# Logits of tiles 12 and 13 by matmuls, a denser order of the early routing's steps, two buffers for the copies of transposed tiles

## The chip, the core and the metric

One NeuronCore of a Trainium2 chip runs the whole program. The metric is the device time of one execution in microseconds; of a kernel the median of its runs is taken. TensorE does matmuls and transposes, VectorE and ScalarE the elementwise work, GpSimd elementwise work and the issue of some DMAs, SyncE the issue of the other DMAs. Each engine takes its instructions in the order in which the program gives them; where one needs another's result it waits on a semaphore, and everything behind it on that engine waits too.

## The reference

Three layers follow each other on 2304 tokens of width 512: a linear attention with a norm for each head, a dense mixture of 4 experts, and a mixture of 8 experts in which each token goes to one.

```python
kv  = einsum('bhsd,bhse->bhde', k, v)
out = einsum('bhsd,bhde->bhse', q, kv)
x   = out / sqrt(mean(out*out, -1) + 1e-6) * g_norm          # -> (2304, 512)
p   = domain_probs / (domain_probs.sum(-1) + 1e-9)
x   = sum_e p[:, e] * (relu(x @ w1[e]) @ w2[e])              # 4 experts, all tokens
xn, en = x / (|x| + 1e-6), emb / (|emb| + 1e-6)
logits = xn @ en.T / tau                                     # 2304 x 8
idx    = argmax(logits, 1);  gate = softmax(logits)[idx]
out[idx == e] = gate * (relu(x[idx == e] @ w1b[e]) @ w2b[e]) # 8 experts
```

## The kernel before

**Tiles.** A tile is 128 tokens, 18 in all (0 to 17); a unit is three tiles, u0 to u5. Tiles 12 to 14 are the fifth unit, u4, tiles 15 to 17 the last, u5. Fp32 operands are split into a high and a low part (`split`: ScalarE casts the high part, as `w1h`, `w2h`, `xth`; VectorE subtracts, as `w1l`, `w2l`, `xtl`, L62), and each product is three matmuls.

**The dense layer** goes expert by expert. A *phase* takes one unit (or a pair, by a Strassen scheme) through one half `fh` of the hidden width. The last four phases belong to the last expert and go (u4, fh0), (u4, fh1), (u5, fh1), (u5, fh0). Each has four *plain steps* (`plain_unit`, L802: 12 matmuls of 128x384; then ScalarE writes `hh`, VectorE `hl`) and six *L2 steps* (`l2_unit`, L909: 6 matmuls of 128x512), two for each tile, part 0 and part 1. Behind part 1 VectorE adds the product to the tile's sum `acc` (L918). When a tile has its last expert's last half (u4 in its fh1, u5 in its fh0) this is final: GpSimd's queue writes the row to `x1d` in DRAM, and a generator for the tile's logits is put into the list `bg`. For tiles 15 to 17 the sum goes to a buffer of its own, `fin`.

**Logits** come in two ways. `logits_v` reads the row back by a DMA from `x1d` and makes eight multiply-reduce operations on VectorE (L314). `logits_t` squares the row on ScalarE, transposes it with four TensorE transposes into `pslt` (L324), copies it to `xx` on ScalarE (L325), and after a `yield` makes the logits by matmuls with 8 columns into `psl` (L329).

**Early routing.** `route_a` stands in `bg` behind the logits of tile 14 and routes the first 15 tiles (TA = 15) while u5 is still in the dense layer: `pick` (largest logit, one-hot `oh`), `ranks` (prefix counts by matmuls, `psr`, L393), `experts` (`e_int`, the expert of each slot, for which SyncE's weight loads of the slots wait), `places`, the gates, then `invert`. `invert` makes the table of which token is in which slot: VectorE writes five one-hot tiles `po` at a time, TensorE multiplies them in `psi` (L454), and VectorE copies the result to `gs` and `ix`. `psl`, `psr` and `psi` share one PSUM buffer (tag `kv`). `route_b` does the like for the last three tiles, later.

**What sets the order.** After each step of a phase `background(pace)` runs so many pieces of the generators in `bg`, up to their next `yield`. A `yield` of a positive number w ends the call and lets the next w calls pass; a `yield -1` only ends the call. The pace is a list, one number a step; after the last phase the rest runs until four slots' stakes are set. The attention of later tiles lies in the phases of the dense layer too: `att` lists units for a tile (`qt_unit` with `psq`, `xt_unit` with `psxt` of the tile before, `x_unit` with `psx`, `x_norm` with VectorE's `xs`), and `spread` puts them at equal distances over a phase.

**The routed layer** takes slots of 128 gathered tokens: GpSimd gathers rows `xg` (L711, by `ix`), TensorE transposes them (`pstx`, L1170), multiplies (`psm`, L1180), transposes the hidden part (`psth`, L1191) and multiplies again (`psy`, L1202). Its weights go through the same split; VectorE's and ScalarE's splits of the first slots are emitted where the program comes to them, between the generators' pieces.

Of the kernel before, what the change touches and what calls it, by code (L numbers as in the profile page):

```python
# [8 lines left out]
F32 = mybir.dt.float32  # L9
# [11 lines left out]
def attn_moe_moe_kernel(ctx: ExitStack, tc: tile.TileContext, q, k, v, g_norm, dprobs, w1, w2, emb, tau, w1b, w2b, out):  # L21
# [4 lines left out]
    D = H * DH  # L26
# [4 lines left out]
    NC = D // 128  # L31
# [3 lines left out]
    TS = SUB // 128  # L35
# [40 lines left out]
    late = {}  # L76
# [101 lines left out]
    def x_norm(t):  # L178
        ps, xs, st = x_rt.pop(t)
        ri = rms_end(*st)  # L180
        nc.vector.tensor_tensor(out=xs, in0=ps, in1=ri.unsqueeze(2).to_broadcast([128, H, DH]), op=ALU.mult)
        x_s[t] = xs
# [33 lines left out]
    TA = 5 * TS  # L216
# [100 lines left out]
            yield 0  # L317

    def logits_t(t, x):
        xx = late["tmp"].tile([128, NC, 128], F32, name="xx", tag="xx")  # L320
        nc.scalar.activation(out=xx.rearrange("p c n -> p (c n)"), in_=x, func=ACTF.Square, accum_out=ssq[:, t:t + 1])
        ps = psp.tile([128, NC, 128], F32, name="pslt", tag=f"x{t % 2}" if t < NT - 1 else nxt("l2"))
        for c in range(NC):
            nc.tensor.transpose(ps[:, c], x[:, 128 * c:128 * c + 128], ident)  # L324
        nc.scalar.copy(xx, ps)  # L325
        yield -1
        pl = psp.tile([128, E2], F32, name="psl", tag="kv")
        for c in range(NC):
            nc.tensor.matmul(out=pl, lhsT=xx[:, c], rhs=en_t[:, c], start=(c == 0), stop=(c == NC - 1))  # L329
        nc.vector.tensor_copy(lg[:, t], pl)  # L330
        yield 0
# [96 lines left out]
    def invert(t1, k0, n, slot):  # L428
        sh = [128, t1, n]
        g = slice(0, t1)  # L430
        so, rhs = tmp(sh, "so", BF16), tmp([128, t1, 5, n], "rhs", BF16)
        gp, ga, gb = tmp([128, 3, t1], "gp", BF16), tmp([128, t1], "ga"), tmp([128, t1], "gb")
        nc.vector.tensor_copy(gp[:, 0], gate[:, g])
        tt(ga, gate[:, g], gp[:, 0], ALU.subtract)
        nc.vector.tensor_copy(gp[:, 1], ga)
        tt(gp[:, 2], ga, gp[:, 1], ALU.subtract)
        tt(so, bc(slot, sh, 2), bc(lane[:, 0:n], sh, 1), ALU.is_equal)
        yield 0
        for i, a in enumerate((ids[:, 0, g], ids[:, 1, g], gp[:, 0], gp[:, 1], gp[:, 2])):
            tt(rhs[:, :, i], so, bc(a, sh, 2), ALU.mult)  # L440
            yield 0
        yield 3
        ps = psp.tile([128, 5, n], F32, name="psi", tag="kv")
        pend = []
        t0 = 0
        while t0 < t1 or pend:
            m = min(R, t1 - t0)
            po = None
            if m:
                po = late["tmp"].tile([128, R, 128], BF16, name="po", tag="po", bufs=2)  # L450
                for i in range(m):
                    ts(po[:, i], lane_b, pos[:, t0 + i:t0 + i + 1], ALU.is_equal)
            for t, w in pend:
                nc.tensor.matmul(  # L454
                    out=ps.rearrange("p a k -> p (a k)"), lhsT=w, rhs=rhs[:, t].rearrange("p a k -> p (a k)"), start=(t == 0), stop=(t == t1 - 1)
                )
            pend = [(t0 + i, po[:, i]) for i in range(m)]
            t0 += m
            yield -1
        sl = slice(k0, k0 + n)  # L460
        nc.vector.tensor_copy(gs[:, sl], ps[:, 0])
        nc.vector.scalar_tensor_tensor(out=ix[:, sl], in0=gs[:, sl], scalar=PAD, in1=ps[:, 1], op0=ALU.add, op1=ALU.add)
        nc.vector.tensor_copy(gs[:, sl], ps[:, 2])
        for i in (3, 4):
            tt(gs[:, sl], gs[:, sl], ps[:, i], ALU.add)
        yield 0
# [431 lines left out]
    def l2_unit(t, e, fh, part, i, first):  # L898
        if part == 0:
            ps2[0] = bank(i)  # L900
        ps = ps2[0]
        u, n = divmod(t % (2 * TS), TS)
        ns = slice(128 * n, 128 * n + 128)
        fs = (0, 1, 3, 2)
        for k in (2 * part, 2 * part + 1):
            f = fs[k]
            j, a = divmod(f, 2)
            for m, (o, w) in enumerate(((0, w2h), (0, w2l), (1, w2h))):
                nc.tensor.matmul(out=ps, lhsT=h_t[o][f][u][:, ns], rhs=w[j][:, a], start=(k == 0 and m == 0), stop=(k == 3 and m == 2))  # L909
        if part == 0:  # L910
            return
        ac = acc[t % len(acc)]
        last = e == E1 - 1 and fh == ((t // TS) % 2 == 0 or t < N // 128 - 2 * TS)
        if first:
            nc.scalar.activation(out=ac, in_=ps, func=ACTF.Copy, scale=dp[:, t, 0:1])
        else:
            fin = late["tmp"].tile([128, D], F32, name="fin", tag="fin", bufs=3) if last and t >= TA else ac
            nc.vector.scalar_tensor_tensor(out=fin, in0=ps, scalar=dp[:, t, e:e + 1], in1=ac, op0=ALU.mult, op1=ALU.add)  # L918
            ac = fin
        if last:  # L920
            nc.gpsimd.dma_start(out=x1d[128 * t:128 * t + 128, :], in_=ac)
            bg.append((logits_v if t < TA - 1 else logits_t)(t, ac))
            if t == TA - 1:
                bg.append(route_a())
            if t == NT - 1:
                bg.append(route_b())

    bg, rest = [], [0]
# [32 lines left out]
    def att(tiles):  # L961
        u, prev = [], None
        for t in tiles:
            u.append(lambda t=t: qt_unit(t))
            if prev is not None:
                u.append(lambda t=prev: xt_unit(t))
            u.append(lambda t=t: x_unit(t))
            u.append(lambda t=t: x_norm(t))
            prev = t
        u.append(lambda: xt_unit(prev))  # L970
        return u
# [99 lines left out]
    def plain_phase(un, e, fh, todo, pace):  # L1071
        steps = [(P1T / 4, lambda f=f: plain_unit(un % 2, f)) for f in range(4)]
        steps += l2_steps(e, fh, [un], None, first_half, (P2T - P1T) / 6)
        run_steps(steps, todo, pace)

    def w2_fills(e, fh, t0=0, t1=P1T):
        return spread([lambda n=n: fill_w2(e, 2 * fh + n) for n in range(2)], t0, t1)

    def w1_plain_fills(e, fh):
        n = 2 * fh  # L1080
        return (
            [(7.9, lambda: w1_blocks(e, n)), (12.0, lambda: w1_blocks(e, n + 1))]
            + spread(plain_direct(n), 8.5, 12) + spread(plain_direct(n + 1), 12.1, 16)
        )
# [33 lines left out]
    for at_ph, ph in enumerate(strassen):  # L1118
        p, e, fh = ph
# [20 lines left out]

    e, u = E1 - 1, UNITS - 2
    plain_phase(u, e, 0, w2_fills(e, 0) + w1_plain_fills(e, 1), [1] * 99)
    plain_phase(u, e, 1, w2_fills(e, 1), [1] * 99)
    plain_phase(u + 1, e, 1, w1_plain_fills(e, 0), [2] * 99)
    todo = w2_fills(e, 0) + [(7.5, lambda: late.update(slots=True)), (8.3, lambda: late.update(weights=True))]
    plain_phase(u + 1, e, 0, todo, [4] * 9 + [0])
    while stake[0] < 4:
# [163 lines left out]
```

## Time and profile before

| | |
|---|---|
| median of 3 runs | 1153.49 us (1151.42 to 1154.02) |
| profiled execution | 1154.61 us, span 1152.70 us |
| TensorE busy | 1110.8 us, 96% of the span |
| VectorE, ScalarE, GpSimd busy | 764.9, 559.5, 276.4 us |
| mean granted TensorE clock | 0.989 |

The span is what the profiler shows of the execution from the first to the last instruction. "Idle before" a row of a timeline is the time in which the engine stood still just ahead of it, with what ended it. A granted clock of 1.00 is 2.4 GHz, 0.50 is 1.2 GHz.

### The profile page before, as it was taken

The page shows a single profiled execution, that of the slowest core. Times are in us where ns is not written, and L with a number is a line of the kernel's source. Part 1 is how long each engine was busy: PE and PEld are TensorE (multiplying, and loading weights), DVE is VectorE, ACT ScalarE, POOL GpSimd, SP SyncE. Part 2 cuts the span into 40 slices and gives each one's busy share as a digit, 9 for nine tenths or more (in the row PEclk, how much of TensorE's full clock was granted, in tenths as well). Part 3 has the DMA queues.
Part 4 walks back from the last instruction along what each step waited for, and adds up shares of the span by engine and source line. Part 5 has one row for each costly group of instructions (what it writes and reads, how often), then busy time and mean ns, then how long its engine had stood idle before and what let it go on. Part 6 is the DMA issues. An engine that isn't in the chain of part 4 may idle for free. (4 is left out here: it accounts for less than half of the span.)

```text
span 1152.7 us, 17304 instructions
## 1 busy us (share of the span) xinstructions
PE 1110.8 (96%) x5905; PEld 972.7 (84%) x5905; DVE 764.9 (66%) x1340; ACT 559.5 (49%) x1000; POOL 276.4 (24%) x325
## 2 busy tenths in 40 slices
PE   7999999999999999999999999999968999999996
PEld 7889898888888898889889998899857878888875
DVE  3467665566996788766796787765876548763662
ACT  3545446444455344444455444332336348763663
POOL 3002332222441322322243322200011112112111
PEclk9999999999999999999999999999989999999999
DMA  9523244221334232221232222123164159855871
GB/s 263 142 55 110 83 147 149 72 82 47 107 113 142 88 92 63 67 74 56 82 119 83 82 83 65 55 73 119 37 240 135 38 163 376 315 172 169 281 239 43
DMA packets 89730, 141.79 MB, mean 123 GB/s; under 512 B 17365, under 2 KB 52181, under 8 KB 89504
## 3 DMA queue, kind: packets, MB, share of 16 engines
q1 hardware_dynamic: 82032, 115.66, 31.1%
q0 software_dynamic: 7600, 24.93, 6.5%
q8 instruction: 49, 0.80, 0.3%
q14 instruction: 49, 0.40, 0.1%
HBM read 178.31 MB, written 10.49 MB: 164 GB/s over the span
## 5 line engine op out<-in xcount | busy, mean ns | idle before, releaser
L909 PE MATMUL bank<-w2h,hh 128*128 128x512 f32 x576 | 227.4, 395 | 1.4 <-ACT hh L786 1.4
L909 PE MATMUL bank<-w2h,hl 128*128 128x512 f32 x576 | 225.5, 391 | 0.0
L909 PE MATMUL bank<-w2l,hh 128*128 128x512 f32 x576 | 225.0, 391 | 0.0
L62 DVE TENSOR_TENSOR w2l<-raw,w2h 128x1024 fp32r<-128x1024 f32 x100 | 120.3, 1225 | 91.5 <-ACT w2h L61 90.9
L814 PE MATMUL bank<-xth,w1h 128*128 128x384 f32 x560 | 145.9, 341 | 5.5 <-ACT s L821 2.6
L814 PE MATMUL bank<-xth,w1l 128*128 128x384 f32 x560 | 142.6, 335 | 0.0
L814 PE MATMUL bank<-xtl,w1h 128*128 128x384 f32 x560 | 142.5, 335 | 0.0
L918 DVE SCALAR_TENSOR_TENSOR acc<-bank,dp,acc 128x512 f32<-128x512 f32 x123 | 91.9, 747 | 59.9 <-PE bank L909 59.6
L909 PEld LDWEIGHTS bank<-w2h,hl 128*128 128x128 f32 x576 | 108.1, 188 | 24.8 <-DVE hl L789 1.8
L909 PEld LDWEIGHTS bank<-w2h,hh 128*128 128x128 f32 x576 | 108.2, 188 | 24.5 <-ACT hh L786 3.7
L909 PEld LDWEIGHTS bank<-w2l,hh 128*128 128x128 f32 x576 | 108.2, 188 | 21.0
L814 PEld LDWEIGHTS bank<-xth,w1h 128*128 128x128 f32 x560 | 99.3, 188 | 11.0 <-ACT s L821 3.8
L62 DVE TENSOR_TENSOR w1l<-raw,w1h 128x512 fp32r<-128x512 f32 (+2 forms) x137 | 89.5, 669 | 22.5 <-ACT w1h L61 22.5
L61 ACT CAST w2h<-raw 128x1024 fp32r<-128x1024 f32 x100 | 102.9, 1056 | 1.8 <-DMA raw<-in_moe_w_dram 0.8
L814 PEld LDWEIGHTS bank<-xtl,w1h 128*128 128x128 f32 x560 | 101.4, 188 | 0.0
L814 PEld LDWEIGHTS bank<-xth,w1l 128*128 128x128 f32 x560 | 101.2, 188 | 0.0
L825 POOL TENSOR_TENSOR sv<-sv,s 128x384 f32<-128x384 f32 x40 | 45.8, 1145 | 202.0 <-ACT sv L821 193.2
L314 DVE CUSTOM_DVE_ANT_0 scr<-row,en_b 128x512 bf16<-128x512 f32 x112 | 86.5, 772 | 9.3 <-DMA row<-x1d 8.8
L821 ACT COPY s<-bank 128x384 f32<-128x384 f32 x80 | 38.3, 479 | 83.2 <-PE bank L814 83.1
L1207 POOL DMA_INDIRECT out_dram<-y,ix x22 | 22.6, 1025 | 223.1 <-ACT y L1206 104.0
L61 ACT CAST w1h<-raw 128x512 fp32r<-128x512 f32 (+2 forms) x140 | 73.9, 572 | 0.0
L61 ACT CAST w1h<-wsum 128x1024 fp32r<-128x1024 f32 x40 | 41.9, 1048 | 63.2 <-POOL wsum L609 63.2
(255 smaller groups left out, 1990.6 us busy)
## 6 DMA issues: line engine op xcount, KB each, us to landing
raw<-in_moe_w_dram SPq DMA_DIRECT2D x290, 512.0 KB
x1d<-acc POOLq DMA_DIRECT2D x15, 256.0 KB, 2.3
row<-x1d POOLq DMA_DIRECT2D x14, 256.0 KB, 3.1
raw<-in_k_dram SPq DMA_DIRECT2D x12, 256.0 KB
raw<-in_v_dram SPq DMA_DIRECT2D x12, 256.0 KB
qraw<-in_q_dram POOLq DMA_DIRECT2D x12, 256.0 KB, 3.9
en_b<-in_moe_expert_emb_dram POOLq DMA_DIRECT2D x1, 2048.0 KB
en_b<-in_k_dram SPq DMA_DIRECT2D x4, 256.0 KB
```

Source lines behind the costliest of these rows:

```text
L61: nc.scalar.copy(hi, raw)
L62: (eng or nc.vector).tensor_tensor(out=lo, in0=raw, in1=hi.bitcast(F32), op=ALU.subtract)
L314: nc.vector.tensor_tensor_reduce(out=scr, in0=x, in1=en_b[:, e], scale=1.0, scalar=0.0, op0=ALU.mult, op1=ALU.add, accum_out=lg[:, t, e:e + 1]
L814: nc.tensor.matmul(out=ps, lhsT=wform(wo, b, w)[:, c], rhs=xform(xo, x)[:, c], start=start and n == 0, stop=(n == 5), skip_group_check=True)
L821: nc.scalar.copy(t, src)
L825: (eng or nc.vector).tensor_tensor(out=out, in0=a, in1=b, op=ALU.add)
L909: nc.tensor.matmul(out=ps, lhsT=h_t[o][f][u][:, ns], rhs=w[j][:, a], start=(k == 0 and m == 0), stop=(k == 3 and m == 2))
L918: nc.vector.scalar_tensor_tensor(out=fin, in0=ps, scalar=dp[:, t, e:e + 1], in1=ac, op0=ALU.mult, op1=ALU.add)
L1207: nc.gpsimd.indirect_dma_start(out=out[:, :], out_offset=bass.IndirectOffsetOnAxis(ap=ix[:, col(s):col(s) + 1], axis=0), in_=y, in_offset= ...
```

## The change

The logits of tiles 12 and 13 are made as tile 14's are, by `logits_t`; `xx` has two buffers; `fin` has two instead of three. In `invert` the `yield 3` is a `yield -1`. In `att` an empty unit follows each `x_norm`, so that `spread` puts the units of a tile at other places of the phase. Two phases get other paces: (u4, fh1) two pieces instead of one after each L2 step, (u5, fh1) three instead of two after each plain step.

```diff
--- before.py
+++ after.py
@@ -317,7 +317,7 @@
             yield 0
 
     def logits_t(t, x):
-        xx = late["tmp"].tile([128, NC, 128], F32, name="xx", tag="xx")
+        xx = late["tmp"].tile([128, NC, 128], F32, name="xx", tag="xx", bufs=2)
         nc.scalar.activation(out=xx.rearrange("p c n -> p (c n)"), in_=x, func=ACTF.Square, accum_out=ssq[:, t:t + 1])
         ps = psp.tile([128, NC, 128], F32, name="pslt", tag=f"x{t % 2}" if t < NT - 1 else nxt("l2"))
         for c in range(NC):
@@ -439,7 +439,7 @@
         for i, a in enumerate((ids[:, 0, g], ids[:, 1, g], gp[:, 0], gp[:, 1], gp[:, 2])):
             tt(rhs[:, :, i], so, bc(a, sh, 2), ALU.mult)
             yield 0
-        yield 3
+        yield -1
         ps = psp.tile([128, 5, n], F32, name="psi", tag="kv")
         pend = []
         t0 = 0
@@ -914,12 +914,12 @@
         if first:
             nc.scalar.activation(out=ac, in_=ps, func=ACTF.Copy, scale=dp[:, t, 0:1])
         else:
-            fin = late["tmp"].tile([128, D], F32, name="fin", tag="fin", bufs=3) if last and t >= TA else ac
+            fin = late["tmp"].tile([128, D], F32, name="fin", tag="fin", bufs=2) if last and t >= TA else ac
             nc.vector.scalar_tensor_tensor(out=fin, in0=ps, scalar=dp[:, t, e:e + 1], in1=ac, op0=ALU.mult, op1=ALU.add)
             ac = fin
         if last:
             nc.gpsimd.dma_start(out=x1d[128 * t:128 * t + 128, :], in_=ac)
-            bg.append((logits_v if t < TA - 1 else logits_t)(t, ac))
+            bg.append((logits_v if t < TA - TS else logits_t)(t, ac))
             if t == TA - 1:
                 bg.append(route_a())
             if t == NT - 1:
@@ -966,6 +966,7 @@
                 u.append(lambda t=prev: xt_unit(t))
             u.append(lambda t=t: x_unit(t))
             u.append(lambda t=t: x_norm(t))
+            u.append(lambda: None)
             prev = t
         u.append(lambda: xt_unit(prev))
         return u
@@ -1140,8 +1141,8 @@
 
     e, u = E1 - 1, UNITS - 2
     plain_phase(u, e, 0, w2_fills(e, 0) + w1_plain_fills(e, 1), [1] * 99)
-    plain_phase(u, e, 1, w2_fills(e, 1), [1] * 99)
-    plain_phase(u + 1, e, 1, w1_plain_fills(e, 0), [2] * 99)
+    plain_phase(u, e, 1, w2_fills(e, 1), [1] * 4 + [2] * 6)
+    plain_phase(u + 1, e, 1, w1_plain_fills(e, 0), [3] * 4 + [2] * 6)
     todo = w2_fills(e, 0) + [(7.5, lambda: late.update(slots=True)), (8.3, lambda: late.update(weights=True))]
     plain_phase(u + 1, e, 0, todo, [4] * 9 + [0])
     while stake[0] < 4:
```

The first place is TensorE in the L2 steps of phase (u4, fh1). This is a piece of the difference; acc_119 is the sum of tile 12, and the matmuls L909 of it are tile 13's part 0 and the beginning of its part 1.

```order
+L324 MATMUL pslt<-ident,acc_119 128x128 x4
+L909 MATMUL bank<-w2h_85,hh_125 128x512
+L909 MATMUL bank<-w2l_87,hh_125 128x512
+L909 MATMUL bank<-w2h_85,hl_133 128x512
+L909 MATMUL bank<-w2h_85,hh_127 128x512
+L909 MATMUL bank<-w2l_87,hh_127 128x512
+L909 MATMUL bank<-w2h_85,hl_135 128x512
+L329 MATMUL psl<-en_t,xx 128x8 x4
+L909 MATMUL bank<-w2h_86,hh_131 128x512
```

The transposes of tile 12 stand directly behind its own last L2 matmul, and its `psl` one part later. Tile 13 (acc_120) has the same; the transposes of tile 14 (acc_121), which stood in the plain steps of the last phase, follow directly on its last L2 matmul too, ahead of the next phase.

The second place is VectorE at the end of the last phase. Before (acc_124 is tile 17, `fin` the final sum):

```order
L918 SCALAR_TENSOR_TENSOR fin<-bank,dp,acc_124 128x512
L338 TENSOR_SCALAR po<-lane_b,pos 128x128 x15
L461 COPY gs<-psi 128x8
L462 SCALAR_TENSOR_TENSOR ix<-gs,psi 128x8
L463 COPY gs<-psi 128x8
L334 TENSOR_TENSOR gs<-gs,psi 128x8 x2
L62 TENSOR_TENSOR xtl<-raw,xth 128x1024 x4
L334 TENSOR_TENSOR xgl<-pstx,xgh 128x512
```

In the changed kernel (acc_122, acc_123 and acc_124 are tiles 15 to 17):

```order
L789 SCALAR_TENSOR_TENSOR hl_140<-bank,hh_132 128x384
L338 TENSOR_SCALAR po<-lane_b,pos 128x128 x5
L918 SCALAR_TENSOR_TENSOR fin<-bank,dp,acc_122 128x512
L461 COPY gs<-psi 128x8
L462 SCALAR_TENSOR_TENSOR ix<-gs,psi 128x8
L463 COPY gs<-psi 128x8
L334 TENSOR_TENSOR gs<-gs,psi 128x8 x2
L62 TENSOR_TENSOR xtl<-raw,xth 128x1024 x4
L918 SCALAR_TENSOR_TENSOR fin<-bank,dp,acc_123 128x512
L330 COPY lg<-psl 128x8 x2
L918 SCALAR_TENSOR_TENSOR fin<-bank,dp,acc_124 128x512
L334 TENSOR_TENSOR xgl<-pstx,xgh 128x512
```

All `po` now stand ahead of tile 15's `fin`, and the copies of `psi` and the four splits `xtl` of the first slot's weights between tile 15's `fin` and tile 16's; before, they stood behind all three.

The third place is TensorE there. Before, behind the last matmuls of `psi`:

```order
L1170 MATMUL pstx<-ident,xg_5479 128x128 x4
L324 MATMUL pslt<-ident,fin 128x128 x4
L1180 MATMUL psm_7580<-xth,xgh 128x512
L1180 MATMUL psm_7580<-xtl,xgh 128x512
L1180 MATMUL psm_7580<-xth,xgl 128x512
```

In the changed kernel, from the end of tile 16's part 0:

```order
L909 MATMUL bank<-w2h_85,hl_136 128x512
L324 MATMUL pslt<-ident,fin 128x128 x4
L909 MATMUL bank<-w2h_86,hh_132 128x512
L909 MATMUL bank<-w2l_88,hh_132 128x512
L909 MATMUL bank<-w2h_86,hl_140 128x512
L909 MATMUL bank<-w2h_86,hh_130 128x512
L909 MATMUL bank<-w2l_88,hh_130 128x512
L909 MATMUL bank<-w2h_86,hl_138 128x512
L329 MATMUL psl<-en_t,xx 128x8 x4
L324 MATMUL pslt<-ident,fin 128x128 x4
L909 MATMUL bank<-w2h_85,hh_126 128x512
```

The transposes of tiles 15 and 16 (`fin`) stand among the L2 matmuls, where before they stood among the first `psm`. `psi` has gone further ahead, in three groups of five: one behind the third plain step, one behind the fourth, one behind tile 15's part 0. `pstx` of the first slot comes behind tile 17's last L2 matmul. `psr` of `route_b`, before behind the second slot's `psth`, comes behind 18 of the second slot's 24 `psm`, and the `oh` that it reads stands on VectorE behind the four splits `w2l` of the first slot.

## Rows read from the trace of the kernel before

**Rows 1.** The page, engines: busy us, share of the span, instructions.
```profile
PE 1110.8 (96%) x5905; PEld 972.7 (84%) x5905; DVE 764.9 (66%) x1340; ACT 559.5 (49%) x1000; POOL 276.4 (24%) x325
```

**Rows 2.** Waits of TensorE, whole run: total us, times, longest us.
```profile
PE psi L454 <- DVE po L338: 5.2, 1, 5.2
PE pstx L1170 <- DMA xg<-x1d,ix: 4.1, 1, 4.1
PE psxt L204 <- DVE xs L181: 3.9, 3, 1.4
PE psl L329 <- ACT xx L325: 3.2, 3, 2.4
```

**Rows 3.** Windows: busy us and count by engine, granted clock, DMA share, GB/s.
```profile
26.00:32.00 6.00, 5.09 (x28) 4.64 (x28) 1.77 (x4) 1.43 (x3) 1.68 (x7) 0.50 0.91 224
...
60.00:80.00 20.00, 18.59 (x102) 16.67 (x102) 11.21 (x24) 7.70 (x13) 0.88 (x1) 1.00 0.25 66
...
875.50:879.00 3.50, 3.50 (x10) 2.73 (x9) 0.36 (x2) 0.00 (x0) 0.00 (x0) 0.51 1.05 403
```

**Rows 4.** Timeline of TensorE around the turn: start us, length us, [idle before].
```profile
799.06 0.39 PE L909 MATMUL bank<-w2h,hh 128*128 128x512 f32 x1
...
807.26 0.87 PE L802 MATMUL bank<-xth,w1h 128*128 128x384 f32 x4
...
825.91 0.60 PE L324 MATMUL pslt<-ident,acc 128*128 128x128 f32 x4
...
831.91 0.85 PE L802 MATMUL bank<-xth,w1h 128*128 128x384 f32 x4
...
833.99 0.39 PE L909 MATMUL bank<-w2h,hh 128*128 128x512 f32 x1
...
848.54 2.49 PE L454 MATMUL psi<-rhs,po 128*128 128x40 bf16 x15 [5.18 <-DVE po L338]
...
855.09 1.11 PE L1170 MATMUL pstx<-ident,xg 128*128 128x128 f32 x4 [4.06 <-DMA xg<-x1d,ix]
...
856.88 0.79 PE L1180 MATMUL psm<-xth,xgh 128*128 128x512 f32 x1
...
873.80 1.06 PE L329 MATMUL psl<-en_t,xx 128*128 128x8 f32 x8 [2.41 <-ACT xx L325]
...
879.13 0.39 PE L1202 MATMUL psy<-w2h,hth 128*128 128x512 f32 x1
...
886.02 0.40 PE L393 MATMUL psr<-oh,ones 128*128 128x24 f32 x2
```

**Rows 5.** Timeline of VectorE around the turn.
```profile
802.02 0.75 DVE L918 SCALAR_TENSOR_TENSOR acc<-bank,dp,acc 128x512 f32<-128x512 f32 x1 [1.68 <-PE bank L909]
...
833.57 1.22 DVE L62 TENSOR_TENSOR w2l<-raw,w2h 128x1024 fp32r<-128x1024 f32 x1 [0.38 <-ACT w2h L61]
...
848.24 2.52 DVE L338 TENSOR_SCALAR po<-lane_b,pos 128x128 bf16<-128x128 bf16 x15
...
851.94 4.65 DVE L62 TENSOR_TENSOR xtl<-raw,xth 128x1024 fp32r<-128x1024 f32 x4
...
869.48 4.63 DVE L62 TENSOR_TENSOR w2l<-raw,w2h 128x1024 fp32r<-128x1024 f32 x4
```

**Rows 6.** Timeline of TensorE, `psxt` of tiles 3, 5 and 8.
```profile
53.29 0.66 PE L204 MATMUL psxt<-ident,xs 128*128 128x128 f32 x4 [1.45 <-DVE xs L181]
...
71.79 0.63 PE L204 MATMUL psxt<-ident,xs 128*128 128x128 f32 x4 [1.41 <-DVE xs L181]
...
212.21 0.63 PE L204 MATMUL psxt<-ident,xs 128*128 128x128 f32 x4 [1.00 <-DVE xs L181]
```

**Rows 7.** Lines of VectorE: busy us, mean ns, idle before.
```profile
L314 DVE CUSTOM_DVE_ANT_0 scr<-row,en_b 128x512 bf16<-128x512 f32 x112 | 86.5, 772 | 9.3 <-DMA row<-x1d 8.8
```

**Rows 8.** Waits of SyncE's queue, 780 to 880 us.
```profile
SPq L720 <- DVE pa L334: 39.2, 1, 39.2
```

**Rows 9.** Timeline of ScalarE around the turn.
```profile
848.82 1.04 ACT L61 CAST xth<-raw 128x1024 fp32r<-128x1024 f32 x1 [0.20 <-DMA raw<-in_moe_w_dram]
```


## The prediction, made before the changed kernel ran

> **What bounds the kernel now.** I read the page's engine line first: TensorE is busy 1110.8 of 1152.7 us [rows 1], so all that it idles is 41.9 us, and a change that leaves the arithmetic alone can only move these 41.9, the clock, or the small matmuls put between the large ones. The waits of TensorE come next [rows 2]: the reader is to see that the two longest single ones, 5.2 us for `po` and 4.1 us for the gathered rows `xg`, have nothing to do with the experts' arithmetic. The windows [rows 3] tell where the clock is at its lower level, 1.2 instead of 2.4 GHz. In TensorE's own timeline [rows 4] both long waits lie between the last L2 matmul of the dense layer and the first `psm` of the routed layer: `psi` stands after all of phase (u5, fh0), and it waits until VectorE has written all fifteen `po` (2.52 us) behind the last tile's `fin` [rows 5]. So the turn between the layers is where the time is. From the end of the third plain step of the last phase (the fourth starts at 831.91) to the first `psy` at 879.13 it takes 47.22 us [rows 4].
>
> **The sum is made against the profiled execution**, 1154.61 us, which is 1.12 above the median 1153.49; its span is 1152.70 with 1.91 around it. A difference is taken over to the median as it is. Less than about 0.2%, 2.3 us, a measurement of this kernel can't tell from nothing.
>
> **Attention: -1.2.** The empty unit moves the other units within `spread`. Three `psxt` wait for VectorE's `xs`: 1.45, 1.41, 1.00 [rows 6]. For tile 3 `x_norm` now stands ahead of a sum (0.45 less), for tile 5 ahead of an accumulation of L918 (0.65 less), and tile 8 gets 36 instead of 30 matmuls between `psx` and `psxt`, which is more than its 1.00. Against that, in tile 4 `psx` now stands directly behind `psq` and waits for ScalarE's copy of `qT`, which before lay behind a plain unit: I take 0.9, from the 1.0 to 1.5 that the like waits cost [rows 6]. Together -1.2; bounds -2.5 (tile 4 free) and +0.5 (only tile 8 gains).
>
> **Tiles 12 and 13 on TensorE: +5.6.** VectorE loses 16 reductions of 772 ns [rows 7]; nothing on the path waited for them, so this is worth nothing by itself. TensorE gains four transposes and the short `psl` matmuls for each tile. For tile 14, now, the two cost 6.00 us for two plain steps (825.91 to 831.91); a plain step is 2.08 (831.91 to 833.99), so 1.84, of which some 0.4 is a wait and its drain [rows 4]: 1.4 without. The pace [2]*6 also puts `pslt(t)` directly behind tile t's own last L2 matmul. It needs VectorE's accumulation, which began 0.04 after the end of tile 12's last matmul and took 0.75 [rows 5]: with the way there and back TensorE stands still some 1.1 us, three times. An accumulation that finds a weight split on VectorE waits up to 0.7 more; none can be below 0.75. So 3 x (1.1 + 1.4) = 7.5, less the 1.84 that tile 14 no longer costs in the last phase: +5.6 (4.6 to 7.7). `psr` of the fifteen tiles now comes at the end of phase (u5, fh1)'s plain steps, with its `oh` long done: +0.5 there.
>
> **The turn: -8.6 at full clock.** An L2 step is 36 matmuls in 8.20 us (799.06 to 807.26), so 1.37 for six [rows 4]. Counted from the end of plain step 3: `psi` is fifteen in 2.49 at the lower clock [rows 4], so 0.43 for five at the upper one. Step 4 ends at 2.5. The second five need `po` behind the split of `w2l` (833.57 to 834.79 before, 1.66 to 2.88 from our zero) [rows 5] and end at 3.8, a new wait of 1.0. Tile 15's parts and the last five: 7.1. Then tile 16's part 0, `pslt` of 15, part 1 and `psl`: 11.1. `pslt` of 16 wants `fin` of 16, and this stands on VectorE behind four splits `xtl` (4.65 us) and the copies of `ix` (0.9, from the end of `psi` at 851.03 to 851.94) [rows 4, 5]: 7.1 + 0.2 + 0.7 + 0.9 + 4.6 + 0.7 = 14.2. TensorE waits 3.0 us. Tile 17's two parts, `psl`, `pstx`: 18.7; `pslt` of 17 waits 0.5 for its `fin`, and the first `psm` is at 19.6. Before it was at 856.88, 24.97 from zero [rows 4]: 5.4 gained, though L2 of the three tiles and the transposes are as many as before. The gathers no longer wait for the last `fin`: they stand on GpSimd right behind the write of tile 15 and have over 8 us for what took 4.1 too long [rows 2].
>
> From the first `psm` to the first `psy` before: 22.25 [rows 4], with 2.4 of waiting for `xx` [rows 2] and 1.7 lost to the lower clock. After it: 48 `psm` at 0.23 are 11.0, `pstx` and `psth` 1.3, one `psl` 0.9, `psr` of the last three tiles 0.5, and waits of 0.7 and 1.0 for `xgh` and `xgl`, 0.3 for `hn`, 0.3 for the slower first matmuls behind these, and a new wait: that `psr` is now behind only 18 `psm` of the second slot, while its `oh` stands on VectorE behind four splits `w2l` that end at 874.11, 17.2 after the first `psm` [rows 4, 5]. ScalarE has 1.2 less ahead of them (`xx` of tile 16 lies earlier) and `oh` takes 1.2 more, so TensorE waits from about 14.1 to 17.2: 3.1. Sum 19.1, 3.2 less than 22.25. The turn is -5.4 - 3.2 = -8.6. `psr` at 886.02 goes from there too: -0.5 [rows 4].
>
> **The clock: +1.7.** After the wait of 2.4 us for `xx` the `psm` from 875.5 to 879.0 ran at a granted clock of 0.51, and at 880 it was full again: 3.5 us at half speed, 1.7 lost [rows 3, 4]. Waits of 1.41 left the clock at 1.00 [rows 3, 6]; so I price waits of 3 us at 1.7 each and those of 1.1 at nothing. There are two such (for `fin` of 16, for `oh`). What the first loses, VectorE's and ScalarE's chain ahead of `oh` partly hides, so I count one. The rule that speaks against this: the Trainium skill, "TensorE: Matmul & The Clock Gate", section "HAM oscillation — how this bites in real kernels", says that an engine that pauses long enough to be counted idle starts again at the low clock, and pays for it at each such pause. By that rule both would be paid, and the sum is 1.7 higher than by counting one; the trace shows one payment behind the one wait of 2.4 us, and agrees so far.
>
> Sum: -1.2 + 5.6 + 0.5 - 8.6 - 0.5 + 1.7 = -2.5; 1154.61 - 2.5 = 1152.1 for the profiled execution, 1151.0 for the median.
>
> The two buffers of `xx` free the second tile's square from waiting for the first tile's `psl`; in the new order each `psl` comes before the next `pslt`, so nothing. Two `fin` instead of three: tile 17's `fin` wants tile 15's buffer, whose write and `pslt` are over by 11, and it comes at 18: nothing, unless the write takes 7 us longer.
>
> **Rivals.**
> *No payment to the clock* (0.20): both waits are short enough, or filled by short matmuls: -4.2, 1149.3. For it: 1.45 and 1.41 cost nothing; against it: 2.4 did.
> *Both paid* (0.27): -0.8, 1152.7. For it: the second wait ends after a stretch of full work, as that of 2.4 us did.
> *Slower: the three waits of 1.1 us in the u4 phase bring the clock down* (0.14). They lie 4.1 us apart. Early in the kernel, after two short waits within 4 us, it was at 0.50 from 26 to 32 [rows 3]. If here too, some 7 us at half speed cost 3.5, and with the same sensitivity both long waits are paid: -0.8 + 3.5 = +2.7, 1156.2. It decides if the clock falls after the second or third of these waits. Against it: the stretches between them are full work.
> *Weights late, so the first wait is longer* (0.04): SyncE's queue now starts the first slot's load earlier (it waited 39.2 us for `e_int` [rows 8]), and the last cast of `xth`, at 848.82 before [rows 9], moves to about 8 from zero; the chain wants it at 12. The fourth load waits for the `w2l` buffer freed at 2.9; only if it needs more than 8 us to land, each us beyond is lost: 2 us more give 1153.0.
>
> **Chances.** My forecast of one payment has 0.35, 1151.0, with its own range 1149.5 to 1152.7 by the bounds of the first two terms. No payment is nearly all faster than 1151.2; of my forecast a little over half; of both paid a tenth: 0.18 + 0.21 + 0.03, and a little for waits that turn out shorter: faster 0.44. Slower than 1155.8 is most of the slower rival and a little of both paid with the bounds against it: 0.13. The same: 0.43. The range 1148.2 to 1155.2 leaves out 0.08 below and 0.12 above.
>
> **What would show it.** Right: no `psi` or `pstx` among the longest waits; three waits of about 1.1 us of `pslt` for `acc` in the u4 phase; one of 3 us of `pslt` for `fin` with `xtl` ahead of it on VectorE; one of about 3 of `psr` for `oh`; first `psm` about 19.6 us after plain step 3; the granted clock below 1.00 in one stretch of that turn. Wrong: a clock below 1.00 in the u4 phase (then slower); a `pslt` wait in the u4 phase near 0.75 or near 1.8 (B is off by 1 to 2); a wait for the raw weights ahead of `xtl`; waits of `psxt` as long as before.

## The result: slower by half a per cent

| | before | changed |
|---|---|---|
| median, 9 runs each on the same chip | 1152.68 us | 1158.40 us (1154.81 to 1163.52) |
| profiled execution, its span | 1154.61, 1152.70 us | 1160.00, 1158.2 us |
| mean granted clock of the profiled execution | 0.989 | 0.987 |

The ratio is 1.0052 (95% interval 1.0034 to 1.0070). The forecast was 1151.0, with 1148.2 to 1155.2 as its range. The two profiled executions differ by 5.4 us, about as much as the medians, so the traces can be subtracted. About 0.7 us of the 5.5 of the spans is chance: the changed one holds a stretch at half clock, at 567.8, that no other trace of the case holds (its price is worked out below).

The waits of TensorE in the changed kernel, whole run, as in [rows 2] (total us, times, longest us):

```profile
PE bank L814 <- ACT s L821: 5.0, 4, 2.4
PE pslt L324 <- DVE fin L918: 3.4, 2, 2.9
PE psi L454 <- DVE po L338: 2.8, 1, 2.8
PE pslt L324 <- DVE acc L918: 2.5, 3, 0.8
PE psr L393 <- DVE oh L334: 2.5, 1, 2.5
...
PE psm L1181 <- ACT xgh L1172: 0.9, 1, 0.9
...
PE psm L1181 <- DVE xgl L334: 0.8, 1, 0.8
PE psx L159 <- ACT qT L148: 0.7, 1, 0.7
```

The two waits of before for `po` after all L2 and for the gathered `xg` are gone. What stands there instead is to be read in TensorE's timeline, as in [rows 4]:

```profile
824.90 0.38 PE L393 MATMUL psr<-oh,ones 128*128 128x120 f32 x2
...
839.12 0.86 PE L802 MATMUL bank<-xtl,w1h 128*128 128x384 f32 x4
842.80 0.84 PE L454 MATMUL psi<-rhs,po 128*128 128x40 bf16 x5 [2.83 <-DVE po L338]
...
844.27 1.46 PE L802 MATMUL bank<-xth,w1l 128*128 128x384 f32 x4
...
857.65 0.89 PE L324 MATMUL pslt<-ident,fin 128*128 128x128 f32 x4 [2.94 <-DVE fin L918]
...
864.47 0.66 PE L324 MATMUL pslt<-ident,fin 128*128 128x128 f32 x4 [0.47 <-DVE fin L918]
...
881.72 0.55 PE L393 MATMUL psr<-oh,ones 128*128 128x24 f32 x2 [2.50 <-DVE oh L334]
...
885.23 0.40 PE L1203 MATMUL psy<-w2h,hth 128*128 128x512 f32 x1
```

The first `psi` begins at 842.80, behind the third plain step (whose last matmuls begin at 839.12 and are issued in 0.69), after 2.83 us of waiting. The second four matmuls of the next plain step, at 844.27, take 1.46 us instead of 0.86. The windows of the changed kernel, as in [rows 3], say why (busy us and count by engine, granted clock, DMA share, GB/s):

```profile
332.30:335.70 3.40, 3.40 (x10) 2.72 (x9) 3.19 (x8) 2.27 (x5) 0.54 (x2) 0.50 0.32 77
567.80:571.20 3.40, 3.40 (x10) 3.11 (x11) 3.27 (x6) 0.94 (x3) 1.37 (x1) 0.50 0.00 0
826.00:843.40 17.40, 14.57 (x74) 12.69 (x73) 16.04 (x65) 6.87 (x14) 0.00 (x0) 1.00 0.22 67
844.30:847.70 3.40, 3.40 (x16) 2.99 (x15) 1.58 (x7) 0.59 (x2) 0.00 (x0) 0.50 0.61 172
857.90:861.30 3.40, 3.40 (x13) 2.83 (x11) 0.00 (x0) 1.04 (x3) 0.58 (x1) 0.50 1.02 320
881.80:885.20 3.40, 3.40 (x10) 2.85 (x11) 0.83 (x5) 0.00 (x0) 0.00 (x0) 0.50 0.85 302
```

Five stretches of 3.4 us have a granted clock of 0.50 and a TensorE without a gap in them: two in the dense layer, three at the turn between the layers. (The stretch from 26 to 32 us in [rows 3], and one at the very end, are in both kernels.) Before there were two, both at the turn: the 3.4 us from 875.5 in [rows 3], and 10.2 us from 848.2, for 4.1 of which TensorE stood idle and waited for the gather. Most of the longer one is in this window of the kernel before:

```profile
848.00:858.00 10.00, 5.40 (x26) 4.02 (x27) 8.83 (x26) 3.39 (x7) 3.51 (x4) 0.51 0.56 191
```

VectorE in the changed kernel, around the turn:

```profile
838.47 0.74 DVE L918 SCALAR_TENSOR_TENSOR acc<-bank,dp,acc 128x512 f32<-128x512 f32 x1
...
840.32 1.21 DVE L62 TENSOR_TENSOR w2l<-raw,w2h 128x1024 fp32r<-128x1024 f32 x1
...
842.03 0.55 DVE L789 SCALAR_TENSOR_TENSOR hl<-bank,hh 128x384 fp32r<-128x384 f32 x1
842.50 0.89 DVE L338 TENSOR_SCALAR po<-lane_b,pos 128x128 bf16<-128x128 bf16 x5
...
850.77 0.75 DVE L918 SCALAR_TENSOR_TENSOR fin<-bank,dp,acc 128x512 f32<-128x512 f32 x1 [1.77 <-PE bank L909]
...
852.30 4.63 DVE L62 TENSOR_TENSOR xtl<-raw,xth 128x1024 fp32r<-128x1024 f32 x4
856.85 0.74 DVE L918 SCALAR_TENSOR_TENSOR fin<-bank,dp,acc 128x512 f32<-128x512 f32 x1
```

Where the 5.5 us of the span are, stretch by stretch, read as differences of starts in the two timelines of TensorE (the last phase's step 3 ends at 831.91 before and at 839.81 now):

| stretch | before | changed | difference | forecast |
|---|---|---|---|---|
| start to the last four phases | 774.16 | 776.15 | +2.0 | -1.2 |
| (u4, fh0), (u4, fh1) to its plain steps' end | 24.90 | 24.89 | 0.0 | 0 |
| (u4, fh1), L2 steps | 8.20 | 14.53 | +6.3 | together +8.0 |
| (u5, fh1), plain steps | 8.34 | 9.70 | +1.4 | |
| (u5, fh1), L2 steps | 8.20 | 8.27 | +0.1 | 0 |
| last phase, plain steps 1 to 3 | 8.11 | 6.27 | -1.8 | -1.8 |
| from there to the first `psy` | 47.22 | 45.42 | -1.8 | -6.9 |
| first `psy` to the end | 273.6 | 273.0 | -0.6 | -0.5 |

### The profile page after: what moved, and what is told of

The parts are those of the page before. It is cut to its first block, busy times and chain, and to the rows that moved or that the text cites. A ratio compares the mean times of both kernels' runs of the same rounds, so it can differ in the third digit from the quotient of the medians.

```text
span 1158.2 us, 17317 instructions
## 1 busy us (share of the span) xinstructions
PE 1116.8 (96%) x5929; PEld 978.4 (84%) x5929; DVE 752.0 (65%) x1310; ACT 559.7 (48%) x1002; POOL 278.9 (24%) x323
## 5 line engine op out<-in xcount | busy, mean ns | idle before, releaser
L909 PE MATMUL bank<-w2h,hh 128*128 128x512 f32 x576 | 230.1, 400 | 1.4 <-ACT hh L786 1.4
L909 PE MATMUL bank<-w2h,hl 128*128 128x512 f32 x576 | 226.6, 393 | 0.0
L909 PE MATMUL bank<-w2l,hh 128*128 128x512 f32 x576 | 226.3, 393 | 0.0
L814 PE MATMUL bank<-xth,w1h 128*128 128x384 f32 x560 | 146.1, 341 | 6.2 <-ACT s L821 5.0
L814 PE MATMUL bank<-xtl,w1h 128*128 128x384 f32 x560 | 143.0, 336 | 0.0
L814 PE MATMUL bank<-xth,w1l 128*128 128x384 f32 x560 | 142.8, 336 | 0.0
L909 PEld LDWEIGHTS bank<-w2h,hl 128*128 128x128 f32 x576 | 109.0, 189 | 24.9 <-DVE hl L789 1.5
L909 PEld LDWEIGHTS bank<-w2h,hh 128*128 128x128 f32 x576 | 109.2, 190 | 24.5 <-ACT hh L786 3.6
L909 PEld LDWEIGHTS bank<-w2l,hh 128*128 128x128 f32 x576 | 109.3, 190 | 20.9
L814 PEld LDWEIGHTS bank<-xth,w1h 128*128 128x128 f32 x560 | 99.6, 188 | 11.4 <-ACT s L821 6.3
L62 DVE TENSOR_TENSOR w1l<-raw,w1h 128x512 fp32r<-128x512 f32 (+2 forms) x137 | 93.2, 692 | 21.9 <-ACT w1h L61 21.6
L814 PEld LDWEIGHTS bank<-xtl,w1h 128*128 128x128 f32 x560 | 101.7, 188 | 0.0
L814 PEld LDWEIGHTS bank<-xth,w1l 128*128 128x128 f32 x560 | 101.4, 188 | 0.0
L821 ACT COPY s<-bank 128x384 f32<-128x384 f32 x80 | 38.3, 479 | 82.4 <-PE bank L814 82.3
L314 DVE CUSTOM_DVE_ANT_0 scr<-row,en_b 128x512 bf16<-128x512 f32 x96 | 74.3, 774 | 2.4 <-DMA row<-x1d 2.1
```

The costliest lines, as they stand in the source:

```text
L62: (eng or nc.vector).tensor_tensor(out=lo, in0=raw, in1=hi.bitcast(F32), op=ALU.subtract)
L314: nc.vector.tensor_tensor_reduce(out=scr, in0=x, in1=en_b[:, e], scale=1.0, scalar=0.0, op0=ALU.mult, op1=ALU.add, accum_out=lg[:, t, e:e + 1]
L814: nc.tensor.matmul(out=ps, lhsT=wform(wo, b, w)[:, c], rhs=xform(xo, x)[:, c], start=start and n == 0, stop=(n == 5), skip_group_check=True)
L821: nc.scalar.copy(t, src)
```

## The experiments

The theory: three things are wrong in the sum, the attention's sign, the work of VectorE ahead of the first `psi`, and how often the clock is paid. Each run was forecast before it ran; there T is what this theory forecasts and R what its rival does. The runs were made on several chips, so a kernel's ratio to before, measured on the same chip, is compared rather than its time.

**Attention alone, undone and done alone.** In the first the line is taken out of the changed kernel, in the second it is put into the kernel before.

```diff
             u.append(lambda t=t: x_norm(t))
-            u.append(lambda: None)
```

> The changed kernel without the empty unit in att; all else as changed. Theory T (the two traces subtracted): the moved attention units cost +2.0 us of the +5.5, above all by the 2.4 us wait for ScalarE's copy s at 331 us and the 3.4 us at half clock behind it. So 1.1 to 2.0 us less than the changed kernel, no wait over 1.2 us on L814, and the granted clock at 1.00 from 320 to 345. Rival R (the prediction's term): the moved units gain 1.2 us, so this one is 1.2 us slower than the changed kernel.

> The kernel before with the empty unit in att and nothing else. T: 1 to 2 us slower than before (0.1 to 0.2%), with the 2.4 us wait on L814 near 331 us. R: 1.2 us faster.

Measured: without it 1156.99 us, 1.0047 (1.0033 to 1.0060) of before, where the changed kernel was 1.0052; with it alone 1154.20, 1.0021 (1.0008 to 1.0033). The long wait on L814 is there with the line alone (2.35 us) and not without it. R falls by the second run: the moved units cost, where it said that they gain 1.2. The price is less sure, 0.6 us by the first run and 2.4 by the second; the first is below T's 1.1 to 2.0, and its interval overlaps that of the changed kernel. The place is the phase that holds the attention of tiles 10 and 11; ScalarE, in the changed kernel:

```profile
327.87 0.58 ACT L173 ACTIVATE xs<-psx 128x512 f32<-128x512 f32 x1
329.73 0.30 ACT L186 ACTIVATE rs<-ms,eps 128x8 f32<-128x8 f32 x1 [1.28 <-DVE ms L175]
...
330.72 0.47 ACT L821 COPY s<-bank 128x384 f32<-128x384 f32 x1
```

and TensorE:

```profile
331.24 0.62 PE L814 MATMUL bank<-xth,w1h 128*128 128x384 f32 x2 [2.36 <-ACT s L821]
```

ScalarE's `rs` of the attention (L186) waits 1.28 us for VectorE's `ms`, and the copy of `s` (L821), for which TensorE's next bank waits, stands behind it. One step of order earlier, and 2.36 us of TensorE went, and with them, in this trace, a stretch of 3.4 us at the lower clock. With the line alone the same wait was there and the clock stayed up:

```profile
328.82 0.62 PE L814 MATMUL bank<-xth,w1h 128*128 128x384 f32 x2 [2.35 <-ACT s L821]
320.00:345.00 25.00, 22.65 (x115) 19.73 (x114) 19.35 (x37) 13.38 (x27) 10.73 (x11) 1.00 0.31 90
```

The predicted gains were there too (0.82 instead of 1.41, nothing instead of 1.00 in tile 8), but for tile 3 only 1.31 instead of 1.45.

**Logits of tiles 12 and 13 back on VectorE.**

```diff
-            bg.append((logits_v if t < TA - TS else logits_t)(t, ac))
+            bg.append((logits_v if t < TA - 1 else logits_t)(t, ac))
```

> The changed kernel with tiles 12 and 13 back on VectorE's logits (and again three buffers of fin and one of xx, which this order needs); paces, yield -1 and attention stay as changed. This puts psi behind tile 17's part 0, and pslt of 15 to 17 among the psm as before. T: the L2 steps of the u4 phase lose their 6.3 us, psi waits some 1 to 2 us behind tile 17 instead of 5.2, pstx waits some 4 us for its gather; about 1149 us, 9 us less than the changed kernel and 3 to 4 less than before. R (the loss lies in the clock at the turn, not in the work added to the u4 phase): at least one long wait stays at the turn, so the clock falls there again, and the time stays above 1155.

Measured: 1151.91 us, 1.0002 (0.9990 to 1.0014). The 6 us came back, so R is wrong on the time, though a long wait stayed at the turn and the clock fell there for 6.8 us, as R said; and T promised 3 more. Its order brings other waits: 1.39 for `oh`, 1.12 for `hl`, 2.48 and 0.87 for `po`; the waits of before for the gather (4.07) and for `xx` (2.41) are back too. The run undoes two things at once, the logits on TensorE and the place of `psi`, so the 6 us aren't the price of the logits alone.

**The step of psi back.**

```diff
-        yield -1
+        yield 3
         ps = psp.tile([128, 5, n], F32, name="psi", tag="kv")
```

> The changed kernel with yield 3 again ahead of psi (and three buffers of fin and one of xx). Tiles 12 and 13 stay on TensorE, paces as changed. psi then comes in groups behind tile 15's part 1, 16's part 0 and part 1, with po on VectorE behind the last hl; the four xtl splits stand three behind fin of 16 and one behind fin of 17; pslt of 15 comes behind pstx. T: the 2.8 us wait for po, the 2.9 us wait for fin and most of the half-clock stretches of the turn go, +6.3 of the u4 phase stays: 1150 to 1152 us, the first psm about 14 us after the third plain step of the last phase. R (yield -1 is what brings psi ahead and pays): as slow as the changed kernel or slower, 1158 or more.

Measured: 1152.31 us, 1.0009 (0.9997 to 1.0021), by the ratios 5 less than the changed kernel, so R is wrong. `psi` costs no wait there; the first `psm` is 17.9 us behind the third plain step, not 14, because T left out the wait for the gather. What is left at the turn are the gather and `xx` of tile 17:

```profile
852.10 0.66 PE L1171 MATMUL pstx<-ident,xg 128*128 128x128 f32 x4 [4.16 <-DMA xg<-x1d,ix]
...
871.13 1.06 PE L329 MATMUL psl<-en_t,xx 128*128 128x8 f32 x8 [2.42 <-ACT xx L325]
```

So with the dense paces and without the `yield -1` the early routing is done in time, and it is the `yield -1` that puts `psi` ahead of what VectorE can deliver. What it saves in turn, these two waits of 6.6 us, it pays with others. Behind the second of the two the clock stayed at 1.00 here (868 to 880 us), where it fell behind the like wait before [rows 3, 4].

**Splits behind the logits of tile 16**, in a generator of their own:

```diff
-        while "weights" not in late:
-            yield 1
-        for n in range(4):
-            slot_split("w1", 0, [n])
-            yield 0
...
+            if t == NT - 2:
+                bg.append(first_splits())
```

> The changed kernel, with the four splits of the first slot's weights put into a generator of their own, begun behind the logits of tile 16 instead of before those of tile 15; all else as changed. fin of 16 then stands on VectorE ahead of all xtl, fin of 17 behind two. T (head of line: fin of 16 is late only because the xtl stand ahead of it): the 2.9 us wait becomes two of 0.8 for fin of 15 and 16, one half-clock stretch of 3.4 us goes; 1155.5 us, 2 to 4 less than the changed kernel. R (VectorE's work is the bound there, whatever its order): the wait comes back as one of 2 us or more of the first psm for xtl, and the time stays within 1 us of the changed kernel's.

Measured: 1159.97 us, 1.0079 (1.0060 to 1.0098): not faster, and rather slower, though the interval overlaps that of the changed kernel; T is wrong on the price. The head of line is as T says (`fin` of 16 waits 0.84 instead of 2.94), but VectorE in this kernel:

```profile
852.04 0.17 DVE L330 COPY lg<-psl 128x8 f32<-128x8 f32 x1 [2.07 <-PE psl L329]
853.54 0.75 DVE L918 SCALAR_TENSOR_TENSOR fin<-bank,dp,acc 128x512 f32<-128x512 f32 x1 [1.34 <-PE bank L909]
857.22 0.17 DVE L330 COPY lg<-psl 128x8 f32<-128x8 f32 x1 [2.93 <-PE psl L329]
857.31 2.36 DVE L62 TENSOR_TENSOR xtl<-raw,xth 128x1024 fp32r<-128x1024 f32 x2
...
860.24 2.35 DVE L62 TENSOR_TENSOR xtl<-raw,xth 128x1024 fp32r<-128x1024 f32 x2
```

It idles for some 6 us between `gs` and the splits, which end at 862.5 instead of 856.9. The first `psm` wait 1.74 for `xgl` behind them, near R's 2 us, and SyncE's next loads, which wait for the splits to free their buffers, are held until 863.0 instead of 857.3. From the first `pstx` to the `psr` that waited for `oh` it is 22.4 us then, 18.3 in the changed kernel. Counted from the start of the last phase, `pstx` itself comes 2.2 us earlier and the first `psy` 0.6 later. The wait for `fin` was exchanged for VectorE's idle time; so moving the splits isn't the mend.

**Transposes of tiles 12 to 14 one step later.**

```diff
         nc.scalar.activation(out=xx.rearrange("p c n -> p (c n)"), in_=x, func=ACTF.Square, accum_out=ssq[:, t:t + 1])
+        if TA - TS <= t < TA:
+            yield -1
```

> The changed kernel, with one yield -1 ahead of the transposes of tiles 12 to 14, so that each stands one step behind its tile's sum; psr, psi and what follows move back by a step too. T: the three waits of 0.84 us for acc go (2.5), and psi's 2.8 us wait with a half-clock stretch goes, since the po have a step more: 1151 to 1153 us. R (the steps are so dense that a wait taken away in the u4 phase comes back at the turn): above 1156.

Measured: 1148.61 us, 0.9966 (0.9949 to 0.9983), faster than T's range, and 0.3% faster than the kernel before. The three waits are gone, as T says: from the L2 steps of (u4, fh1) to the last phase it is 2.9 us less. The wait of `psi` is not: it grew,

```profile
PE psi L456 <- DVE po L340: 3.7, 1, 3.7
...
PE psr L395 <- DVE oh L336: 0.9, 1, 0.9
```

because the `po` come later too (the second split of `w2l` now stands ahead of the first five). It is the wait for `fin` that went, 2.94 to 0.20: this order has three of the splits ahead of `fin` of 16 instead of four, and `pslt` of 16 one part later. So the gain has two causes, of which T had one. The shorter wait for `oh`, 0.9 for 2.50, is no third one: TensorE was at half clock from 868.2 to 871.6 just ahead of it and so came to it later. From the first `psm` to the first `psy` it is 18.71 us here, and 18.75 in the changed kernel with its waits filled (below), where the clock stayed up. So this stretch cost nothing: the wait behind it, for another engine, took it in.

**What the first runs seemed to point to, together**: no empty unit, `yield 1`, and the later splits; then also the later transposes.

> What the first runs point to, together: the changed kernel without the empty unit, with yield 1 ahead of psi (between the -1 and the 3), three buffers of fin and one of xx, and the splits of the first slot begun behind the logits of tile 16. The three waits for acc in the u4 phase stay. T: no wait for po or for the gather, 2 x 0.8 for fin of 15 and 16, some 2.5 for oh: 1147 us (1145 to 1149), ratio to before 0.996. R (the 7.7 us of logits on TensorE can't be won back at the turn): 1152 or more.

> The kernel with yield 1, without the empty unit and with the later splits, and in addition the transposes of tiles 12 to 14 one step later. T: 2.5 us less than without that, by the three waits of 0.84: 1144.5 us (1143 to 1147). R (the u4 phase's waits are free since the turn waits for the same chain): no difference to the one without it.

Measured: 1154.27 us, 1.0014 (1.0000 to 1.0027), and 1155.58, 1.0018 (1.0004 to 1.0033). T is wrong by 7 to 11 us. Both have the later splits, and the waits that these brought above: the first `psm` wait 1.74 and 1.59 for `xgl`, and the clock is at half from 858.7 for 10.2 us in the one, from 858.6 for 6.8 in the other. No run has these orders without the later splits, so that these are the cause is argued and not shown. In these orders the 2.5 us of the u4 phase were no gain (R of the second holds): `psi` waits in both, 2.36 and 2.31.

**The clock by itself.** Empty matmuls of the identity fill the waits, with nothing moved:

```diff
+            if k0 == 0 and pend and pend[0][0] == 0:
+                heat(14, psp.tile([128, 128], F32, name="fill", tag="tp"))
             for t, w in pend:
```

and the like ahead of the other places.

> The changed kernel, with TensorE doing empty matmuls of the identity in its three long waits at the turn: 14 ahead of the first psi, 14 ahead of pslt of tile 16, 12 ahead of psr of the last three tiles (some 0.18 us each); nothing else moves. T (each of these waits brings the clock down for 3.4 us): the granted clock stays at 1.00 in the turn and the time falls by up to 3 x 1.7, to 1153.5 to 1156. R (the clock falls by other causes, or what it loses is hidden by VectorE's chain): within 1 us of the changed kernel.

> The kernel before, with empty matmuls in its own three waits: 26 ahead of psi (5.2 us), 20 ahead of the first pstx (4.1 us), 11 ahead of psl of tile 17 (2.4 us). T: the half-clock stretches 848 to 858 and 875.5 to 879 go: 3 to 4 us less than before, ratio 0.997. R: no difference.

Measured: the changed kernel with fills 1153.09 us, 0.9995 (0.9982 to 1.0009) of before, so 5 to 7 us less than without (5.3 by the medians, 6.6 by the ratios); the kernel before with fills 1150.20, 0.9972 (0.9960 to 0.9984). Windows of the first:

```profile
843.00:847.00 4.00, 4.00 (x26) 3.35 (x25) 3.33 (x13) 1.71 (x3) 0.00 (x0) 1.00 0.64 213
856.00:860.00 4.00, 4.00 (x26) 3.50 (x24) 0.17 (x1) 1.12 (x3) 0.59 (x1) 1.00 1.00 319
877.00:881.00 4.00, 4.00 (x29) 3.64 (x27) 1.96 (x9) 0.42 (x1) 0.00 (x0) 1.00 0.74 227
```

and its timeline, from the first fill to the first `psy`:

```profile
839.12 3.29 PE L988 MATMUL fill<-ident 128*128 128x128 f32 x28
842.25 0.73 PE L460 MATMUL psi<-rhs,po 128*128 128x40 bf16 x5
...
880.32 0.39 PE L1209 MATMUL psy<-w2h,hth 128*128 128x512 f32 x1
```

The windows of the kernel before with fills, for the stretches that were at half clock:

```profile
848.00:859.00 11.00, 10.70 (x84) 8.98 (x82) 8.71 (x27) 4.74 (x7) 3.51 (x4) 1.00 0.57 194
872.00:880.00 8.00, 8.00 (x47) 6.82 (x46) 3.08 (x6) 4.21 (x7) 0.00 (x0) 1.00 0.71 252
```

T holds in both: no stretch of the turn is at half clock any more. The changed kernel even fell a little more than T's 5.1, within the intervals. (Fourteen empty matmuls took 3.29 us, 0.23 each, not 0.18.) In the traces the first `psy` of the changed kernel comes 4.9 us earlier, of which 0.7 was gained ahead of `psi`, by the missing stretch at 567.8; so the three stretches cost some 4.2, 1.4 each, of the 1.7 that each loses on TensorE. Beside the kernel before with fills the changed one with fills is still 2.9 us slower: the order loses by itself, and the clock about doubles that. In these 2.9 is also the stretch at 332 in the dense layer, which was not filled.

**Together, from what held**: the later transposes without the empty unit, then with 18 empty matmuls ahead of the first `psi` as well.

> The kernel with the later transposes of tiles 12 to 14 (else as changed), without the empty unit in att. T: the 2.0 us wait for ScalarE's s near 331 and what clock it costs go, tile 8's 1.0 comes back: 0.5 to 2 us less than with the empty unit, 1147 us. R (the moved attention gains): 1 us more.

> The kernel with the later transposes and without the empty unit, with 18 empty matmuls ahead of the first psi, where TensorE waits 3.7 us for po. T: 6.8 us at half clock behind that wait go, of which some 2 are not hidden by VectorE: 1145 us (1143.5 to 1147). R: no difference to the one without them.

Measured: 1148.30 us, 0.9956 (0.9941 to 0.9972), and 1146.64, 0.9947 (0.9932 to 0.9962). Beside the later transposes with the empty unit (0.9966) the first is faster as T says, but the intervals overlap. The second is the fastest version run, 6 us below the kernel before, and in T's range; but its interval overlaps that of the first too, and in the first's own trace only 3.4 us behind `psi` were at half clock, not 6.8. In the second `psi` waits for nothing and the clock stays up there, with one stretch at half clock left, behind a wait of 2.5 us for `oh`:

```profile
836.00:846.00 10.00, 10.00 (x66) 8.06 (x65) 8.55 (x27) 3.69 (x6) 2.66 (x3) 1.00 0.32 90
869.40:872.80 3.40, 3.40 (x10) 2.62 (x9) 1.17 (x3) 2.57 (x3) 0.00 (x0) 0.50 1.01 354
```

## Why the prediction was wrong

The sum gave -2.5 where the span shows +5.5. The 8 us between them lie in three steps of the sum: the attention, the turn, and the clock.

**"Attention: -1.2" was +2.0 in the trace** (0.6 to 2.4 by the runs). The step priced only the waits that the trace of before shows and one new one. The failure is in what it left out: the units were moved in all phases, and where ScalarE's `rs` waits for VectorE, what stands behind it on ScalarE came late. The forecast's 0.9 for tile 4 was 0.73. The new wait of 2.36 took back the gains, and no more: up to the last four phases TensorE's waits add up to 16.8 us before and to 16.1 in the changed kernel. What makes the +2.0 is above all the clock, which the step put at nothing in the dense layer: the stretches at 332.3 and 567.8. The second is chance. The changed kernel with fills is the same program up to the turn, lacks this stretch, and begins its last phase at 832.86 instead of 833.54. In the traces that have no stretch at half clock at all ahead of the last four phases, these begin at 771.40 with the line, and without it at 770.30 to 770.86 in three and at 773.16 in one; against the three, the line alone costs 0.5 to 1.1 where the clock stays up.

**"Tiles 12 and 13 on TensorE" was right in size**: 8.0 forecast, 7.7 measured, and -1.8 given back in the last phase as forecast. The waits for `acc` are 0.84 each, where 1.1 stood:

```profile
804.81 0.66 PE L324 MATMUL pslt<-ident,acc 128*128 128x128 f32 x4 [0.84 <-DVE acc L918]
```

**"The turn: -8.6 at full clock"** was -6.0 by the kernel with fills (839.12 to 880.32, 41.2 us against 47.22). The wait for `fin` of 16 was 2.94 for 3.0, of 17 0.47 for 0.5, of `xgh` and `xgl` 1.6 for 1.7, of `oh` 2.50 for 3.1. What failed is the first five `po`: the step let them come in time and gave the second five a wait of 1.0; in fact TensorE waits 2.83 us for the first and not at all for the second. It carries through to the first `psm`: in the kernel with fills this is 22.45 us behind the third plain step, where 19.6 stood. From there to the first `psy` the sum was right, 18.75 for 19.1. VectorE was busy 16.0 of the 17.4 us up to there: `psr` stands at 824.90, and all of `places` and the gates is behind it, with the splits of `w1l`, the three tiles' `acc`, `hl` and `w2l` between. `hl` of step 2, which stands just ahead of the first `po`, began at 842.03, 3.5 us after its `hh` was done. The order that was read for this step shows what is ahead of a `po`, not how late VectorE already is; adding up VectorE's rows from `psr` on would have shown it. No run takes work from VectorE ahead of the `po`, so that this backlog makes the wait is read from the trace.

**"The clock: +1.7, I count one"** was three at the turn, 4.2 us, and one or two in the dense layer (at 332 behind the wait of 2.36, at 567.8). The extra wait for `po` made the third. And nothing was hidden of what the stretch behind the wait for `fin` lost: from the first `psm` to the `psr` that waits for `oh` it is 16.84 us with it and 16.86 in the kernel with fills, so the chain ahead of `oh` came later by as much. The Trainium skill, "TensorE: Matmul & The Clock Gate", section "HAM oscillation — how this bites in real kernels", has the restart at the low clock paid at each pause that counts as idle. The changed kernel's trace agrees with it: three waits of 2.5 to 2.9 us at the turn, three stretches at half clock. All traces together don't make it a matter of a wait's length alone: behind waits of 2.3 to 2.5 us the clock fell in 14 of 19 cases (last section). The rival "both paid", 1152.7, was nearer than the forecast; the rival of the slower side, a fall of the clock behind the three short waits of the u4 phase, did not come: from 800 to 826 the clock was at 1.00. Its 1156.2 is the nearest to 1158.40 of the times forecast, but by luck: the kernel was slower by other means than that rival's. Attention off by 3.2, the wait for `po` and the rest of the turn by 2.6, the clock at the turn by 2.5, the others by -0.3: together 8.0.

The experiments show the price of the clock at the turn, of the `yield -1` and of the waits for `acc` (with that for `fin`) each by a run, and that the attention costs; its price stays between 0.6 and 2.4. That the attention's loss is all in the one phase of tiles 10 and 11 is read from the traces alone.

## What to carry to other kernels

When a step is moved ahead, add up the work of the engine that feeds it from the last point where that engine waited, not only the instruction that stands just ahead. A transpose placed directly behind the last matmul of the sum that it reads paid the way through the other engine each time here, 0.84 us of waiting; one step later it waited for nothing. Most of the long waits here (2.3 to 2.9 us) cost TensorE more than their own length, and filling them with empty matmuls is a cheap test of how much of a loss is clock. Before a stretch is priced from one trace, look whether other traces of the same order have it. A wait that is closed on one engine can come back as idle time on another, as when the splits were moved behind the logits of tile 16.

## What the runs showed of the hardware

The spread of the runs goes with the clock. On one chip the kernel before gave 1150.2 to 1152.3 us with a mean granted clock of 0.992, and 1152.2 to 1155.5 at 0.988 and 0.989; the changed one 1154.8 at 0.993 and 1163.5 at 0.986. The same pair of waits (0.46 and 1.1 us near 566) was followed by a stretch of 3.4 us at half clock in one profiled execution and by none in the thirteen others, so that pair pays only sometimes. The same holds for the stretch early in the kernel, 26 to 32 us in [rows 3]: the two waits around its start (1.7 us, and 0.8 to 1.1) are in all fourteen traces, the stretch of 6.8 us in six of them. And it holds for longer waits. Of those of 2.8 to 2.9 us in all traces the clock fell during or soon after each of five; of those of 2.3 to 2.5 us in 14 of 19. The five that cost nothing are the 2.35 for `s` with the empty unit alone, the 2.48 for `po` and the 2.41 for `xx` with tiles 12 and 13 back on VectorE, the 2.42 for `xx` with `yield 3`, and the 2.50 for `oh` with `yield 1` and the later splits. How many stretches the turn holds changes too: without the empty unit the order of the turn is the changed kernel's, with the same waits (2.82, 2.93 and 2.48), but there 20.5 us of it were at half clock instead of 10.2. With the fills the clock's mean rose to 0.998 in some runs of either kernel.
